# Moving the float64 loads and the converted stores of a fused attention and two-MLP kernel from SyncE's queue to ScalarE's, with the conversion's sum in place

## The chip, the cores and the metric

The kernel runs on one core of a Trainium2 chip. The metric is the device time of one execution in microseconds (us), and lower is better. The core has TensorE (PE, with its weight loads as PEld), VectorE (DVE), ScalarE (ACT), GpSimd (POOL) and SyncE (SP), which run their own instruction lists in order and wait for one another by semaphores. DMAs are started by an instruction in the list of an engine; before the change that engine is SP for all of them.

## The reference

An attention with pooled queries is followed by two MLPs over the same 2304 tokens, batch by batch. q, k and v are float32; the four weight matrices are float64.

```python
# batch, n_heads, seq, head_dim = 4, 8, 1152, 64
q_pool = q.reshape(B, H, S // factor, factor, D).mean(axis=3)     # factor = 2
scores = scale * np.matmul(q_pool, k.transpose(0, 1, 3, 2))
scores = scores - np.max(scores, axis=-1, keepdims=True)
attn = np.exp(scores)
attn = attn / (np.sum(attn, axis=-1, keepdims=True) + 1e-09)
return np.matmul(attn, v).astype(np.float32)
...
# moe:  d_model, d_ff = 512, 2048
h = x @ w_in
g = np.maximum(0.01 * h, h)
return (g @ w_out).astype(np.float32)
...
# moe2: same shapes
g = np.where(h > 0.0, h, alpha * (np.exp(np.minimum(h, 0.0)) - 1.0))
return (g @ w_out).astype(np.float32)
```

## The kernel before

Matrix products are made from float32r halves: a float32 operand is split into a high and a low part (`psplit`: the high part by ACT or DVE, the low part by POOL or DVE as a subtraction), and three products (high-high, high-low, low-high) are accumulated where both operands are split. The attention of one pair of heads is nine score tiles: scores on PE (L452), a row maximum on DVE (L457, L459), the exponential on ACT (L463, with the row sum), transposes on PE (L475), a split of the transposed tile by ACT (L261) and DVE (L267), and the product with v (L496). One MLP of one batch runs over 16 blocks `f` of 128 hidden columns: `up` (L629) makes h for one block and the two halves of 288 tokens, ACT and DVE apply the activation (L640 and L642, or L645, L648 and L650), ACT and POOL split it into `g`, and after every fourth block `down` (L667) multiplies by w_out and DVE adds into `acc` (L680).

**Weights.** Every MLP block needs one 128x512 piece of w_in and one of w_out. The first batch of each layer converts them from float64; the later batches reload the converted float32 pieces, which the first stored to DRAM (`kept`). There are 2 layers x 16 blocks x 2 pieces = 64 pieces, and `convert` handles each in two halves of 256 columns, so 128 blocks. For one block: SP loads 256 columns as pairs of 32-bit words into `cr` (L290); DVE makes two passes over the high words into a buffer `ct` (L293, L296); ACT scales the low words in place (L299) and takes the magnitude into `cm` (L301); POOL adds the low part to `ct` (L303); DVE multiplies `ct` by a mask made from `cm` and writes the half of the piece, `wr` (L305). `cr`, `ct` and `cm` have two buffers each (CB). When a piece is complete SP stores it (L328), ACT splits it into the matmul's weight `wi` or `wo` (L261) and POOL makes the low part (L267). `wr` has four buffers, two per block `f`. The five output tiles at the end of each batch also use the tag `cr` for the ACT evictions (L707) that SP then stores (L712).

**Order.** Nothing is in hand order: each step is added to `Program` with an engine, a cost in ns and a rank, and `schedule` lays all steps out with these costs and fixed latencies (a DMA from SP counts 60 ns and lands 2500 ns later; three matmuls of an MLP block count 3 x 123 ns). An engine takes the step of lowest rank that is ready by that plan, and the instructions are written out in the order of the planned starts. On the chip every engine then follows its list in order, whatever the real durations are. In the lists below, `w0_6_0` is the stored piece of layer 0, block 6, w_in (`_1` for w_out), and the numbers behind the names are those of buffers.

Of the kernel before, what the change touches and what calls it, by code (L numbers as in the profile page):

```python
# [36 lines left out]
class Program:  # L37
# [10 lines left out]
    def __init__(self):  # L48
        self.ops, self.tags = [], {}

# [5 lines left out]

    def add(self, engine, cost, rank, fn, w=(), r=()):

        me = len(self.ops)
        deps, starts, frees = set(), set(), []  # L60

        def hits(accesses, part):
            return [o for o, p in accesses if p is None or part is None or p == part]

        for x in r:
            b, part = x if isinstance(x, tuple) else (x, None)
            deps.update(hits(b.writers, part))
            b.readers.append((me, part))
        for x in w:
            b, part = x if isinstance(x, tuple) else (x, None)  # L70
            deps.update(hits(b.writers, part))
            deps.update(hits(b.readers, part))
            if b.first is None:
                b.first = me
            if b.prev is not None:
                frees.append(b.prev)
            if b.before is not None:
                starts.add(b.before)
            b.writers.append((me, part))
        deps.discard(me)  # L80
        self.ops.append((engine, cost, rank, fn, deps, starts, frees))

    def schedule(self):
# [25 lines left out]
        while left:  # L109
# [4 lines left out]
            while again:  # L114
                again = False
                for e in idle:
# [16 lines left out]
                    for o, done in out[i]:  # L133
# [5 lines left out]
                        else:  # L139
                            t = end + self.LATENCY.get(e + " " + e2, self.LATENCY[e])  # L140
                        ready[o] = max(ready[o], t)
                        need[o] -= 1
# [12 lines left out]
def kernel(  # L155
# [36 lines left out]
    CW = 256  # L192
    CB = 2
    CLEAD = 3
# [76 lines left out]
    def convert(rank, dst, src):  # L271
# [6 lines left out]
        for n in range(0, 512, CW):  # L278
            r = sb("cr", [128, CW, 2], U32, CB)
            t = sb("ct", [128, CW], U32, CB)  # L280
            mag = sb("cm", [128, CW], F32, CB)

            def load(n=n, r=r):
                rv = r.ap.rearrange("p n t -> p (n t)")
                if len(src.shape) == 3:
                    k0, kn = n // src.shape[2], CW // src.shape[2]
                    rv, sv = rv.rearrange("p (c n) -> p c n", c=kn), src[:, k0:k0 + kn, :]
                else:
                    sv = src[:, n:n + CW]
                nc.sync.dma_start(out=rv, in_=sv.bitcast(U32))  # L290

            prog.add("SP", 60, rank - 1, load, w=[r])
            prog.add("DVE", dve(CW, True), rank, lambda r=r, t=t: V.tensor_scalar(  # L293
                out=t.ap, in0=r[:, :, 1], scalar1=3, scalar2=0x3FFFFFF8,
                op0=ALU.logical_shift_left, op1=ALU.bitwise_and), w=[t], r=[(r, 1)])
            prog.add("DVE", dve(CW), rank, lambda r=r, t=t: V.scalar_tensor_tensor(  # L296
                out=t.ap, in0=r[:, :, 1], scalar=0xC0000000, in1=t.ap,
                op0=ALU.bitwise_and, op1=ALU.bitwise_or), w=[t], r=[(r, 1), t])
            prog.add("ACT", act(CW, sbuf=True), rank, lambda r=r: A.activation(  # L299
# [3 lines left out]
            prog.add("POOL", pool(CW), rank, lambda t=t, r=r: G.tensor_tensor(  # L303
                out=t.ap, in0=t.ap, in1=r[:, :, 0], op=ALU.add), w=[t], r=[t, (r, 0)])
            prog.add("DVE", dve(CW), rank, lambda n=n, t=t, mag=mag: V.scalar_tensor_tensor(  # L305
                out=dst[:, n:n + CW], in0=mag.ap, scalar=MIN_HI, in1=t.ap.bitcast(F32),
                op0=ALU.is_ge, op1=ALU.mult), w=[(dst, n)], r=[t, mag])

    kept = {}

    def load_w(rank, layer, w_in, w_out, f):

        src = (w_in[:, f * 128:(f + 1) * 128].rearrange("(c p) f -> p c f", p=128),
               w_out[f * 128:(f + 1) * 128, :])
        rs = [sb("wr", [128, 512], F32, WRB) for _ in range(2)]
        for i, r in enumerate(rs):
            if w_in.dtype == F32:
# [7 lines left out]
            else:  # L325
                convert(rank - CLEAD, r, src[i])
                kp = kept[layer, f, i] = Buf(lambda i=i: dram.tile([128, 512], F32, name=f"w{layer}_{f}_{i}"))
                prog.add("SP", 60, rank, lambda r=r, kp=kp: nc.sync.dma_start(out=kp.ap, in_=r.ap), w=[kp], r=[r])  # L328
        wi = sb("wi", [128, 2, DC, 128], F32R, WIB)
        wo = sb("wo", [128, 2, DM], F32R, WOB)  # L330
        psplit(rank - 0.5, WH, WL, lambda: wi[:, 0].rearrange("p c n -> p (c n)"),
               lambda: wi[:, 1].rearrange("p c n -> p (c n)"), lambda: rs[0].ap, 512, (wi, 0), [rs[0]])
        psplit(rank - 0.5, WH, WL, lambda: wo[:, 0], lambda: wo[:, 1], lambda: rs[1].ap, 512, (wo, 0), [rs[1]])
        return wi, wo

# [259 lines left out]
    def mlp(at, span, b, layer, xin, w_in, w_out, tags):  # L595
# [22 lines left out]
        def up(f):  # L618
# [4 lines left out]
            for hf in range(2):  # L623
# [9 lines left out]
                for c in range(DC):  # L633
                    prog.add("PE", 3 * 123, rank + step * hf / 2, lambda h=h, c=c, cols=cols: mm(h, c, cols),
                             w=[h], r=[wi, (xs[c], hf), (xs[c], 2 + hf)])
# [21 lines left out]
        def down(fc):  # L657
            for hf in range(2):
                for d in range(DC):
# [12 lines left out]
                    for f in fs:  # L672
                        prog.add("PE", 3 * 123, rank, lambda f=f, mm=mm: mm(f), w=[y],
                                 r=[w[f][1], (g[f], hf), (g[f], 2 + hf)])
# [94 lines left out]
```

## Time and profile before

| | us |
|---|---|
| median of 3 runs | 1546.47 |
| lowest and highest | 1545.47, 1552.09 |
| the profiled execution's own time | 1545.34 |
| its span, first to last instruction | 1543.5 |
| PE busy (share of the span) | 1414.5 (92%) |
| ACT busy | 1065.9 (69%) |
| DVE busy | 1011.4 (66%) |
| POOL busy | 830.3 (54%) |
| mean busy share of the 16 DMA engines, queue of SP | 28.0% |

The shares are means over stages that differ. The core starts with attention of the first batch and the first conversions; from about 216 to 593 us the two MLPs of the first batch run, with the conversions of the rest of the weights and the attention of the next batch between them; from 606 us on only reloaded weights are used. The chain of work that ended last is PE for 64% of the span and DVE for 21%.

### The profile page before, as it was taken

The page shows a single profiled execution, that of the slowest core. Times are in us where ns is not written, and L with a number is a line of the kernel's source. Part 1 is how long each engine was busy: PE and PEld are TensorE (multiplying, and loading weights), DVE is VectorE, ACT ScalarE, POOL GpSimd, SP SyncE. Part 2 cuts the span into 40 slices and gives each one's busy share as a digit, 9 for nine tenths or more (in the row PEclk, how much of TensorE's full clock was granted, in tenths as well). Part 3 has the DMA queues.
Part 4 walks back from the last instruction along what each step waited for, and adds up shares of the span by engine and source line. Part 5 has one row for each costly group of instructions (what it writes and reads, how often), then busy time and mean ns, then how long its engine had stood idle before and what let it go on. Part 6 is the DMA issues. An engine that isn't in the chain of part 4 may idle for free.

```text
span 1543.5 us, 28953 instructions
## 1 busy us (share of the span) xinstructions
PE 1414.5 (92%) x10288; PEld 1365.2 (88%) x10288; DVE 1011.4 (66%) x2273; ACT 1065.9 (69%) x2901; POOL 830.3 (54%) x840
## 2 busy tenths in 40 slices
PE   5878889888888898999999999999999999899997
PEld 4777788888878887999999999899999998899897
DVE  6999889899998998556565556645665554124222
ACT  6989878776678787676668776676667763443553
POOL 5443255765766667254555556254554445466662
PEclk9999999999999999999999999999999999999999
DMA  4332123343334443222222222222221121322221
GB/s 138 99 115 87 40 75 123 121 130 125 126 118 144 130 143 120 74 71 73 67 69 86 79 78 63 74 76 66 71 67 59 55 56 56 93 76 82 69 82 39
DMA packets 82642, 135.59 MB, mean 88 GB/s; under 512 B 8512, under 2 KB 26944, under 8 KB 82496
## 3 DMA queue, kind: packets, MB, share of 16 engines
q1 hardware_dynamic: 82496, 133.73, 28.0%
q8 instruction: 81, 1.33, 0.4%
q14 instruction: 65, 0.53, 0.1%
HBM read 112.20 MB, written 21.50 MB: 87 GB/s over the span
## 4 chain that ended last, share of the span: by engine, by line
PE 64%; DVE 21%; ACT 6%; issue 3%; DMA 3%; POOL 2%; SPq 0%; ACTq 0%; POOLq 0%; DVEq 0%
PE h L667 17%; PE h L629 16%; PE s L452 8%; PE o L496 7%; PE t L475 5%; DVE m L457 3%; PE s L629 3%; DVE ct L293 3%; DVE wr L305 3%; DVE ct L296 3%; DVE pt L267 2%; PE s L667 2%; PE t L373 2%; PE t L629 2%; PE t L667 2%
## 5 line engine op out<-in xcount | busy, mean ns | idle before, releaser
L667 PE MATMUL h<-g,wo 128*128 128x288 f32 x2544 | 437.1, 302 | 17.5 <-DVE t L650 7.9
L629 PE MATMUL h<-xs,wi 128*128 128x288 f32 x2520 | 429.2, 305 | 22.9 <-DVE t L650 14.2
L629 PEld LDWEIGHTS h<-xs,wi 128*128 128x128 f32 x2520 | 362.5, 190 | 32.5 <-DVE t L650 20.0
L667 PEld LDWEIGHTS h<-g,wo 128*128 128x128 f32 x2544 | 367.1, 188 | 23.8 <-DVE t L650 9.6
L457 DVE TENSOR_REDUCE m<-s 128x1 f32<-128x384 f32 x432 | 232.2, 550 | 74.4 <-PE s L452 71.6
L261 ACT ACTIVATE pt<-t 128x384 fp32r<-128x384 f32 (+1 forms) x416 | 184.0, 457 | 115.2 <-PE t L475 108.3
L463 ACT ACTIVATE p<-s,m 128x384 f32<-128x384 f32 x432 | 249.5, 588 | 18.3 <-DVE m L459 18.0
L267 DVE TENSOR_TENSOR pt<-t,pt 128x384 fp32r<-128x384 f32 (+1 forms) x416 | 206.8, 509 | 73.3 <-ACT pt L261 71.7
L267 POOL TENSOR_TENSOR g<-t,g 128x288 fp32r<-128x288 f32 x256 | 211.1, 831 | 79.9 <-ACT g L261 75.5
L267 POOL TENSOR_TENSOR wo<-wr,wo 128x512 fp32r<-128x512 f32 x128 | 166.4, 1304 | 137.5 <-ACT wo L261 134.3
L452 PE MATMUL s<-kT,qT 128*128 128x384 f32 x768 | 197.0, 354 | 25.4 <-ACT p L463 24.5
L267 POOL TENSOR_TENSOR wi<-wr,wi 128x512 fp32r<-128x512 f32 x128 | 167.6, 1309 | 91.9 <-ACT wi L261 79.3
L496 PE MATMUL o<-pt,vn 128*128 128x256 f32 (+1 forms) x1152 | 192.5, 303 | 5.5 <-DVE pt L267 3.6
L475 PE MATMUL t<-ident,p 128*128 128x128 f32 x1116 | 181.6, 277 | 12.4 <-DVE pt L267 11.7
L496 PEld LDWEIGHTS o<-pt,vn 128*128 128x128 f32 x1152 | 165.5, 190 | 10.6 <-DVE pt L267 10.2
L475 PEld LDWEIGHTS t<-ident,p 128*128 128x128 f32 x1116 | 139.4, 142 | 22.1 <-DVE pt L267 12.3
L452 PEld LDWEIGHTS s<-kT,qT 128*128 128x128 f32 x768 | 125.5, 192 | 32.2 <-ACT p L463 31.0
L303 POOL TENSOR_TENSOR ct<-ct,cr 128x256 uint32<-128x256 uint32 x128 | 98.8, 774 | 96.7 <-DVE ct L296 29.8
L261 ACT ACTIVATE g<-t 128x288 fp32r<-128x288 f32 x256 | 112.2, 445 | 49.0 <-DVE t L650 28.4
L267 POOL TENSOR_TENSOR vn<-raw,vn 128x576 fp32r<-128x576 f32 x32 | 46.4, 1449 | 174.4 <-ACT vn L261 174.4
L261 ACT ACTIVATE wo<-wr 128x512 fp32r<-128x512 f32 x128 | 80.6, 630 | 78.9 <-PE h L667 47.5
L680 DVE TENSOR_TENSOR acc<-h,acc 128x288 f32<-128x288 f32 x158 | 71.1, 452 | 67.2 <-PE h L667 66.1
(106 smaller groups left out, 2080.0 us busy)
## 6 DMA issues: line engine op xcount, KB each, us to landing
wr<-w SPq DMA_DIRECT2D x192, 256.0 KB, 2.6
cr<-in_moe_w_in_dram SPq DMA_DIRECT2D x64, 256.0 KB, 2.7
cr<-in_moe_w_out_dram SPq DMA_DIRECT2D x64, 256.0 KB, 2.7
w<-wr SPq DMA_DIRECT2D x64, 256.0 KB, 2.4
raw<-in_k_dram SPq DMA_DIRECT2D x32, 288.0 KB, 3.0
raw<-in_v_dram SPq DMA_DIRECT2D x32, 288.0 KB, 3.1
raw<-in_q_dram SPq DMA_DIRECT2D x32, 256.0 KB, 2.9
out_dram<-cr SPq DMA_DIRECT2D x16, 256.0 KB, 2.1
```

The costliest lines, as they stand in the source:

```text
L261: prog.add("ACT", act(n, sbuf=not psum), rank, lambda: A.activation(out=hi(), in_=src(), func=ACTF.Copy), w=[w], r=r)
L267: lambda: eng.tensor_tensor(out=lo(), in0=src(), in1=f32(hi()), op=ALU.subtract),
L293: prog.add("DVE", dve(CW, True), rank, lambda r=r, t=t: V.tensor_scalar(out=t.ap, in0=r[:, :, 1], scalar1=3, scalar2=0x3FFFFFF8, op0=ALU.l ...
L303: prog.add("POOL", pool(CW), rank, lambda t=t, r=r: G.tensor_tensor(out=t.ap, in0=t.ap, in1=r[:, :, 0], op=ALU.add), w=[t], r=[t, (r, 0)])
L452: PE.matmul(out=st[:, 0:384], lhsT=qa(a), rhs=kT[:, 384 * c:384 * c + 384], start=(i == 0), stop=(i == len(seq) - 1))
L457: prog.add("DVE", dve(384), rank - LR, lambda st=st, c=c: V.tensor_reduce(out=m[:, c:c + 1], in_=st[:, 0:384], axis=AX.X, op=ALU.max), w=[ ...
L463: prog.add("ACT", act(384, True), rank - LE, lambda c=c: A.activation(out=p[:, 384 * c:384 * c + 384], in_=banks[c][:, 0:384], func=ACTF.E ...
L475: PE.transpose(out=t[:, i, :], in_=p[:, (3 * c + i) * 128:(3 * c + i + 1) * 128], identity=ident)
L496: PE.matmul(out=o[:, 0:n], lhsT=vn[:, c, :], rhs=pt[th][:, a, c % 3, :], start=(c == 3 * ORDER[0] and a == 0), stop=(c == 3 * ORDER[2] + 2 ...
L629: PE.matmul(out=h[:, 0:HB], lhsT=wi[:, a, c, :], rhs=xs[c][:, e, cols], start=(c == 0 and a == 0 and e == 0), stop=(c == DC - 1 and a == 1))
L667: PE.matmul(out=y[:, 0:HB], lhsT=w[f][1][:, a, d * 128:(d + 1) * 128], rhs=g[f][:, e, cols], start=(f % FC == 0 and a == 0 and e == 0), st ...
L680: prog.add("DVE", dve(HB), rank - HURRY, lambda y=y, a_=a_, cols=cols: V.tensor_tensor(out=a_[:, cols], in0=y[:, 0:HB], in1=a_[:, cols], o ...
```

## The change

Three things move, and some of the planner's numbers.

- The load of a float64 block and the store of a converted piece are issued from ACT's list rather than SP's. The planner counts 80 ns of ACT for each, and takes their result as ready 3000 ns later than an ACT result would be (`late`). The store's rank goes from `rank` to `rank - 0.4`, behind the two splits of the same block (`rank - 0.5`), and it is added behind them.
- The buffer `ct` is gone: both DVE passes, the POOL sum and the mask work in the half of `wr` itself. `wr` is thus first written by the first pass and not by the last step.
- `CB` is 3 and not 2: three `cr` buffers, for the loads and for the output tiles. `cm` keeps two.
- Three matmuls of an MLP block count 3 x 133 ns in the planner, in `up` and in `down`, where they counted 3 x 123.

```diff
-    def add(self, engine, cost, rank, fn, w=(), r=()):
+    def add(self, engine, cost, rank, fn, w=(), r=(), late=0):
...
+        if late:
+            self.late[me] = late
...
-                        ready[o] = max(ready[o], t)
+                        ready[o] = max(ready[o], t + self.late.get(i, 0) * done)
...
-    CB = 2
+    CB = 3
...
             r = sb("cr", [128, CW, 2], U32, CB)
-            t = sb("ct", [128, CW], U32, CB)
-            mag = sb("cm", [128, CW], F32, CB)
+            t = lambda n=n: dst[:, n:n + CW].bitcast(U32)
+            mag = sb("cm", [128, CW], F32, 2)
...
-                nc.sync.dma_start(out=rv, in_=sv.bitcast(U32))
-
-            prog.add("SP", 60, rank - 1, load, w=[r])
+                nc.scalar.dma_start(out=rv, in_=sv.bitcast(U32))
+
+            prog.add("ACT", 80, rank - 1, load, w=[r], late=3000)
...
             prog.add("POOL", pool(CW), rank, lambda t=t, r=r: G.tensor_tensor(
-                out=t.ap, in0=t.ap, in1=r[:, :, 0], op=ALU.add), w=[t], r=[t, (r, 0)])
+                out=t(), in0=t(), in1=r[:, :, 0], op=ALU.add), w=[(dst, n)], r=[(dst, n), (r, 0)])
...
-                prog.add("SP", 60, rank, lambda r=r, kp=kp: nc.sync.dma_start(out=kp.ap, in_=r.ap), w=[kp], r=[r])
+                stores.append((kp, r))
...
+        for kp, r in stores:
+            prog.add("ACT", 80, rank - 0.4, lambda r=r, kp=kp: nc.scalar.dma_start(out=kp.ap, in_=r.ap), w=[kp], r=[r],
+                     late=3000)
...
-                    prog.add("PE", 3 * 123, rank + step * hf / 2, lambda h=h, c=c, cols=cols: mm(h, c, cols),
+                    prog.add("PE", 3 * 133, rank + step * hf / 2, lambda h=h, c=c, cols=cols: mm(h, c, cols),
...
-                        prog.add("PE", 3 * 123, rank, lambda f=f, mm=mm: mm(f), w=[y],
+                        prog.add("PE", 3 * 133, rank, lambda f=f, mm=mm: mm(f), w=[y],
```

Two places of the lists show the move. First SP in the middle of the conversions, around blocks 8 and 9 of the first layer; before, the loads of float64 blocks (L290), the loads of k, q and v (L349, `raw`) and the stores of pieces (L328) stand in one row:

```order
L328 DMA w0_8_0_3545<-wr_3490 128x512
L290 DMA cr_3578<-in_moe_w_in_dram 128x2x256
L349 DMA raw_3622<-in_k_dram 128x576
L349 DMA raw_3624<-in_q_dram 128x512
L290 DMA cr_3635<-in_moe_w_in_dram 128x2x256
L328 DMA w0_8_1_3742<-wr_3722 128x512
L290 DMA cr_3770<-in_moe_w_out_dram 128x512
L290 DMA cr_3787<-in_moe_w_out_dram 128x512
L349 DMA raw_3826<-in_v_dram 128x576
L328 DMA w0_9_0_3901<-wr_3887 128x512
```

In the changed kernel SP has at this place only the loads of the attention (the line is now L357):

```order
L357 DMA qrem_3032<-in_q_dram 64x128 x2
L357 DMA raw_3463<-in_v_dram 128x576
L357 DMA raw_3660<-in_k_dram 128x576
L357 DMA raw_3664<-in_q_dram 128x512
L357 DMA raw_3904<-in_v_dram 128x576
L357 DMA raw_4270<-in_k_dram 128x576
```

What left SP's list stands in ACT's. Here is ACT around block 6 before, between the conversion steps (L299, L301), exponentials (L463), splits (L261) and evictions:

```order
L299 ACTIVATE cr_3205<-cr_3205 128x256
L301 ACTIVATE cm_3272<-cr_3205 128x256
L261 ACTIVATE pt_3275<-t_3175 128x3x64
L261 ACTIVATE pt_3029<-t_3253 128x3x64
L463 ACTIVATE p_3243,sum_2704<-s_3181,m_3155 128x384
L261 ACTIVATE pt_3295<-t_3253 128x3x64
L261 ACTIVATE wi_3297<-wr_3128 128x512
L507 ACTIVATE tm_3319<-o_3236 64x320
L299 ACTIVATE cr_3279<-cr_3279 128x256
L301 ACTIVATE cm_3333<-cr_3279 128x256
```

The same place after, where the loads (L293) stand between compute steps and the conversion steps are L302 and L304:

```order
L302 ACTIVATE cr_3192<-cr_3192 128x256
L293 DMA cr_3278<-in_moe_w_out_dram 128x512
L471 ACTIVATE p_3255,sum_2673<-s_3137,m_3127 128x384
L293 DMA cr_3284<-in_moe_w_out_dram 128x512
L304 ACTIVATE cm_3287<-cr_3192 128x256
L515 ACTIVATE tm_3293<-o_3194 64x320
L293 DMA cr_3299<-in_moe_w_in_dram 128x2x256
L471 ACTIVATE p_3255,sum_2673<-s_3166,m_3127 128x384
L264 ACTIVATE pt_3177<-t_3289 128x3x128
L685 ACTIVATE acc_3316<-h_3235 128x288
L264 ACTIVATE pt_3239<-t_3301 128x3x128
L264 ACTIVATE wi_3326<-wr_3079 128x512
```

A load in ACT's list now stands before an exponential or an eviction, which cannot start on ACT until the load has been issued.

## Rows read from the trace of the kernel before

**Rows 1.** The page: busy time by engine, then busy tenths in 40 slices.
```profile
PE 1414.5 (92%) x10288; PEld 1365.2 (88%) x10288; DVE 1011.4 (66%) x2273; ACT 1065.9 (69%) x2901; POOL 830.3 (54%) x840
...
DVE  6999889899998998556565556645665554124222
```
**Rows 2.** Windows: stretch and length; busy us of PE, PEld, DVE, ACT, POOL; clock; DMA.
```profile
0.00:165.00 165.00, 125.10 (x832) 112.91 (x832) 142.59 (x349) 139.67 (x396) 73.28 (x83) 0.97 0.33 104
...
216.00:593.00 377.00, 328.63 (x2313) 307.07 (x2312) 351.62 (x746) 289.36 (x816) 245.41 (x259) 0.99 0.41 130
...
606.00:1543.00 937.00, 905.89 (x6756) 894.45 (x6755) 465.08 (x1060) 583.22 (x1542) 485.35 (x475) 0.99 0.24 70
```
**Rows 3.** Waits of SP's queue, 216 to 593 us: waiter, releaser, us in total, times, longest.
```profile
SPq L290 <- POOL ct L303: 158.7, 102, 4.2
SPq L290 <- ACT cm L301: 52.9, 40, 3.8
```
**Rows 4.** The float64 loads and the stores: issue ns min/median/max; us to landing.
```profile
L290 SPq DMA_DIRECT2D cr<-in_moe_w_in_dram x64: 378/379/587, 4.7 to 578.9; - x64
L290 SPq DMA_DIRECT2D cr<-in_moe_w_out_dram x64: 327/328/579, 13.2 to 585.5; - x64
...
DMA to landing us min/median/max: 2.4/2.7/4.7
...
L328 SPq DMA_DIRECT2D w<-wr x64: 320/327/535, 25.1 to 593.9; - x64
```
**Rows 5.** Chain of waits that ended last within 216 to 593 us, by line.
```profile
by line: DVE ct L296 10.2%; DVE wr L305 10.0%; DVE ct L293 10.0%; issue 7.7%; DVE m L457 7.4%; DVE pt L267 5.7%; PE h L667 4.7%; PE h L629 4.2%; DMA cr<-in_moe_w_out_dram 3.7%; DMA cr<-in_moe_w_in_dram 3.3%; POOL ct L303 2.6%; DVE acc L680 
```
**Rows 6.** DVE's groups, 216 to 593 us: busy us, mean ns | idle before, releasers.
```profile
L305 DVE SCALAR_TENSOR_TENSOR wr<-cm,ct 128x256 f32<-128x256 f32 x107 | 74.3, 698 | 1.5 <-POOL ct L303 1.4
L296 DVE SCALAR_TENSOR_TENSOR ct<-cr,ct 128x256 uint32<-128x256 uint32 x106 | 69.0, 654 | 0.9
L293 DVE TENSOR_SCALAR ct<-cr 128x256 uint32<-128x256 uint32 x106 | 56.6, 537 | 3.6 <-DMA cr<-in_moe_w_in_dram 1.8 <-DMA cr<-in_moe_w_out_dram 1.6
L267 DVE TENSOR_TENSOR pt<-t,pt 128x384 fp32r<-128x384 f32 (+1 forms) x114 | 56.2, 504 | 2.9 <-ACT pt L261 2.7
...
L642 DVE TENSOR_TENSOR t<-h,t 128x288 f32<-128x288 f32 x29 | 13.0, 447 | 5.7 <-ACT t L640 5.7
```
**Rows 7.** ACT's conversion step, 216 to 593 us, in the same form.
```profile
L299 ACT ACTIVATE cr<-cr 128x256 uint32<-128x256 uint32 x104 | 45.8, 440 | 15.3 <-DMA cr<-in_moe_w_out_dram 11.3 <-DMA cr<-in_moe_w_in_dram 2.7 <-POOL wi L267 0.9
```
**Rows 8.** DVE's conversion steps, whole run: ns min/median/max.
```profile
L293 DVE TENSOR_SCALAR ct<-cr x128: 273/294/1514, 7.7 to 589.7; 128x256 uint32<-128x256 uint32 x128
...
L305 DVE SCALAR_TENSOR_TENSOR wr<-cm,ct x128: 402/417/1685, 12.6 to 593.3; 128x256 f32<-128x256 f32 x128
```
**Rows 9.** Timeline around 301 us: start us, us, engine, line (ACT, DVE, POOL).
```profile
301.43 0.43 ACT L301 ACTIVATE cm<-cr 128x256 f32<-128x256 f32 x1
...
304.18 0.43 ACT L299 ACTIVATE cr<-cr 128x256 uint32<-128x256 uint32 x1
304.51 0.42 ACT L301 ACTIVATE cm<-cr 128x256 f32<-128x256 f32 x1
...
301.19 1.51 DVE L293 TENSOR_SCALAR ct<-cr 128x256 uint32<-128x256 uint32 x1
...
300.95 1.61 POOL L267 TENSOR_TENSOR kn<-raw,kn 128x576 fp32r<-128x576 f32 x1
...
303.64 0.74 POOL L303 TENSOR_TENSOR ct<-ct,cr 128x256 uint32<-128x256 uint32 x1 [0.75 <-issue]
```
**Rows 10.** Waits in the first 165 us: waiter, releaser, us in total, times, longest.
```profile
POOL qs L397 <- DMA raw<-in_q_dram: 14.6, 5, 4.0
...
DVE ct L293 <- DMA cr<-in_moe_w_in_dram: 7.0, 4, 5.9
```
**Rows 11.** Timeline: output tiles at 642 us (PE behind the evictions) and at the end.
```profile
644.52 3.71 PE L629 MATMUL h<-xs,wi 128*128 128x288 f32 x15 [1.79 <-ACT cr L707]
...
1538.79 0.60 ACT L707 ACTIVATE cr<-t 128x512 f32<-128x512 f32 x1 [1.49 <-DMA out_dram<-cr]
```

More of the change, by code (lines that the diff above doesn't have):

```diff
@@ L48, in __init__ @@
     def __init__(self):
-        self.ops, self.tags = [], {}
+        self.ops, self.tags, self.late = [], {}, {}
     def buf(self, tag, bufs, make):
@@ L289, in load @@
                     sv = src[:, n:n + CW]
-                nc.sync.dma_start(out=rv, in_=sv.bitcast(U32))
-            prog.add("SP", 60, rank - 1, load, w=[r])
+                nc.scalar.dma_start(out=rv, in_=sv.bitcast(U32))
+            prog.add("ACT", 80, rank - 1, load, w=[r], late=3000)
             prog.add("DVE", dve(CW, True), rank, lambda r=r, t=t: V.tensor_scalar(
-                out=t.ap, in0=r[:, :, 1], scalar1=3, scalar2=0x3FFFFFF8,
-                op0=ALU.logical_shift_left, op1=ALU.bitwise_and), w=[t], r=[(r, 1)])
+                out=t(), in0=r[:, :, 1], scalar1=3, scalar2=0x3FFFFFF8,
+                op0=ALU.logical_shift_left, op1=ALU.bitwise_and), w=[(dst, n)], r=[(r, 1)])
             prog.add("DVE", dve(CW), rank, lambda r=r, t=t: V.scalar_tensor_tensor(
-                out=t.ap, in0=r[:, :, 1], scalar=0xC0000000, in1=t.ap,
-                op0=ALU.bitwise_and, op1=ALU.bitwise_or), w=[t], r=[(r, 1), t])
+                out=t(), in0=r[:, :, 1], scalar=0xC0000000, in1=t(),
+                op0=ALU.bitwise_and, op1=ALU.bitwise_or), w=[(dst, n)], r=[(r, 1), (dst, n)])
             prog.add("ACT", act(CW, sbuf=True), rank, lambda r=r: A.activation(
@@ L303, in convert @@
             prog.add("POOL", pool(CW), rank, lambda t=t, r=r: G.tensor_tensor(
-                out=t.ap, in0=t.ap, in1=r[:, :, 0], op=ALU.add), w=[t], r=[t, (r, 0)])
+                out=t(), in0=t(), in1=r[:, :, 0], op=ALU.add), w=[(dst, n)], r=[(dst, n), (r, 0)])
             prog.add("DVE", dve(CW), rank, lambda n=n, t=t, mag=mag: V.scalar_tensor_tensor(
-                out=dst[:, n:n + CW], in0=mag.ap, scalar=MIN_HI, in1=t.ap.bitcast(F32),
-                op0=ALU.is_ge, op1=ALU.mult), w=[(dst, n)], r=[t, mag])
+                out=dst[:, n:n + CW], in0=mag.ap, scalar=MIN_HI, in1=t().bitcast(F32),
+                op0=ALU.is_ge, op1=ALU.mult), w=[(dst, n)], r=[(dst, n), mag])
     kept = {}
@@ L315, in load_w @@
         rs = [sb("wr", [128, 512], F32, WRB) for _ in range(2)]
+        stores = []
         for i, r in enumerate(rs):
```

## The prediction

> **What bounds the kernel now.** I read the page first: PE is busy for 92% of the span, DVE for 66%, but the slices show DVE at eight to nine tenths and more for the first 15 of 40 and far lower after [rows 1]. So there are two kernels in one. From 606 us on PE is busy 905.9 of 937 us and hardly anything else can matter [rows 2]. Before that DVE is the fuller engine: in the stretch from 216 to 593 us, in which the two MLPs of the first batch run beside the conversions, DVE is busy 351.6 of 377 us (93%), PE 328.6 (87%), ACT 289.4 (77%) [rows 2]. The change touches this stretch, so I took the other views for it alone. The chain of waits there is DVE work in its majority: the three conversion steps L293, L296 and L305 are 30% of it, loads of `cr` 7.0% (26 us), "issue" 7.7% [rows 5]. Of DVE's groups the same three are the costliest, and DVE has in all only 377 - 351.6 = 25.4 us of idle time; 3.6 us of it stands before L293 and ends with a load [rows 6]. ACT waits for the same loads longer: 14.0 us before L299 [rows 7].
>
> SP's own waits say why loads come late. Of the 106 loads in the stretch, 102 waited for POOL's L303, the last reader of the `cr` buffer, 158.7 us in total, and 40 for ACT's L301 [rows 3]. With two buffers a load cannot go out before the block two places ahead is through, and it lands 2.7 us after its issue [rows 4]. The loop of the conversion is thus closed through the buffers, and SP does nothing but wait in it.
>
> **The conversions, 216 to 593 us.** A third `cr` buffer takes a load out of this loop: it can go out one block earlier, and a block takes 377/106 = 3.6 us, more than the landing of 2.7. So the waits for loads should go: 3.6 us on DVE and 14.0 on ACT. DVE's gain is more than its own 3.6, since it waits for ACT steps that stand behind the late L299: 5.7 us before L642 and 2.7 before L267 [rows 6]. 3.6 + 5.7 + 2.7 = 12.0, and I take **-12 us**. The bounds are 0, if DVE's stops merely move to its next wait, and -25, all its idle time. What is late next is DVE itself: its work in the stretch is not shortened by the change. The sum in place removes no instruction; it exchanges `ct` for `wr` in the same five steps. It makes `wr` taken earlier, at the first pass. In the list of the changed kernel the first pass on a `wr` stands behind the store of the piece that held it by 60 and more in the numbers of the buffers, which rise along the lists, so I price that at 0, up to +10 if the store is late.
>
> **The issue on ACT.** 192 issues leave SP and enter ACT's list, 128 loads and 64 stores. On SP one took 379, 328 or 327 ns [rows 4], so 64 x (379 + 328 + 327) = 66 us, some 54 of them in the stretch (106 loads, 53 stores). That is the upper bound, if nothing else of ACT goes on meanwhile. The lower bound is 0: ACT's steps overlap already, as L299 at 304.18 takes 0.43 us and L301 starts 0.33 us after it [rows 9], and an issue of 0.33 to 0.38 us that runs while the step ahead of it works costs next to nothing. The trace has no DMA on ACT, so I cannot tell; I take 0.1 us each, 19 us of ACT's time, nearer the lower end, since ACT is mostly fed and has 88 us of idle time in the stretch. A tenth of that on the path makes **+2 us** (0 to +20). The Trainium skill (Advanced Engine Details and Errata, Engine Queue Depths) gives ScalarE a queue of 8 instructions. By it the issue would be hidden nearly always, and the term would be 0 rather than +2; no row here shows the depth.
>
> **The waits on ACT.** A load still waits for POOL's sum on the buffer, and now ACT stands still for it; behind it are queued exponentials, splits and evictions, for which PE and DVE wait. One block shows the size: L301 ends at 301.86, and POOL's sum (the next L303) ends at 304.38, 2.5 us later [rows 9]. In the changed list the load stands a median of 7 ACT rows behind the last ACT step on the buffer; at 377/816 = 0.46 us a row that is 3.2 us, so the typical load finds the buffer free, but some 30 of 125 stand 5 rows or fewer behind and would wait half a microsecond or so: 15 us of ACT, part of it instead of other waits. I take **+2 us** on the path (0 to +33; the upper end is the rival below). The stores stand behind the splits of the same piece, and only a few of them wait for anything but an old DMA: 0.
>
> **The two engines on one port.** L293 takes 273 ns at best and 537 on average in the stretch, L305 402 and 698 [rows 6, 8], and the row at 301.19 shows how: it lasts 1.51 us, to 302.70, and POOL's L267, begun before it, ends at 302.56 [rows 9]. For three steps (L296 goes like L305) the excess is 106 x (264 + 251 + 296) = 86 us. The Trainium skill (SBUF — State Buffer, Who interferes with whom) tells of an exclusive lock that DVE and GpSimd take in turns, held for a whole instruction; the trace agrees, with 1.51 us for a step of 0.27. What follows from the rows: POOL's 245.4 us of work [rows 2] fill 65% of 377 us, and 68% of 361. So the excess rises with the share, 86 x 68/65 = 90: **+2 us** after what is hidden (-20 to +20, since another order meets other POOL steps).
>
> **The first 216 us, the output tiles, the planner.** SP without float64 loads in its list can fetch q, k and v sooner: POOL waits 14.6 us for q [rows 10], off the chain mostly; against that, three loads from ACT now compete with the first k. **-2 us** (-8 to +2). The third buffer lets an output tile be evicted without waiting for the store two tiles ahead: 1.79 us of PE at 644 us and 1.49 of ACT near the end [rows 11], together **-3 us** (-5 to 0). The cost of 133 in place of 123 changes the plan's idea of PE; behind 606 us, where PE has 31 us of idle time [rows 2], the order of the large groups reads nearly the same, and up to 593 us some nine row maxima fewer stand between the conversions, and come back later. 0 (-5 to +5).
>
> **The sum**, against the profiled execution's own time (span 1543.5 and 1.8 around it, 1545.3): -12 + 2 + 2 + 2 - 2 - 3 = -11, so 1534. The median of the runs, 1546.5, is 1.1 above the profiled execution, so I predict 1535.
>
> **The rivals.**
> *ACT becomes the bound* (slower). If the issues cost their full 54 us in the stretch and each load holds ACT for half of what SP waited (158.7/102/2 = 0.78 us, 83 us for 106), ACT needs 289 + 54 + 83 = 426 us where the stretch has 377: +49. It decides from 88 us in 159 transfers, 0.55 us each, on. Half of it falls into waits that ACT has anyway: +25, with -5 from the other terms 1566. For it: ACT is in order, and 102 of 106 loads waited. Against it: the third buffer and the rows in between.
> *No change.* DVE stays the bound at 93% and only its own 3.6 us and the output tiles are gained, against 4 of ACT: about 1543. The Trainium skill (DMA: Bandwidth & Descriptors, Issuing engines are not separate DMA queues) speaks for it: another issuing engine saves only the sequencer's time to issue. What the rows show is that SP's time is waiting for buffers, not issuing [rows 3], so the second list by itself would give nothing here, and the buffer all.
> *More.* All of DVE's idle time is filled (-25) and the steps meet POOL less often (a quarter of 86 is -20, half of it on the path): 1545 - 35 - 5 = 1510 at the far end, 1518 as its middle.
>
> **How the numbers follow.** Forecast (1526 to 1538) 0.40, more 0.15, no change (1538 to 1553) 0.27, ACT as the bound 0.18. Half a percent, 7.7 us, is about what a measurement of this kernel can tell from no change: faster 0.55, same 0.27, slower 0.18. The range 1512 to 1554 leaves out the end of "more" (0.05) and most of the slow rival (0.14).
>
> **What would show it.** Right: waits of L296 and L302 (the old L293 and L299) for loads near zero; DVE at 95% or more in a stretch some 12 us shorter; ACT's loads issued without long idle time behind them. Wrong: ACT rows behind a load that wait for POOL, 40 us and more in sum; or the stretch as long as before with DVE's waits moved to ACT steps; or the stretch shorter and the time given back behind 606 us, which would be the planner's order. The forecast rests most on DVE's stops being due to late loads by way of ACT.

## The result and the profile after

The changed kernel takes 1558.58 us (1554.74 to 1563.18, 8 runs), the kernel before in the same comparison 1546.64 us. The ratio is 1.0077, with a 95% interval of 1.0055 to 1.0100: 12 us **slower**, where 1535 us were forecast, and 4.6 us outside the range. The profiled execution took 1554.74 us, the lowest of the eight, so its trace (a span of 1553.0 us, 1543.5 before) shows 9.5 of the 12 us. In the code after the change the lines are 3 to 8 higher, the store's 12: loads L293, passes L296 and L299, ACT's steps L302 and L304, POOL's sum L306, mask L308, stores L340.

The page of the changed kernel, busy time by engine, then the queues (q10 is ACT's), beside [rows 1]:

```profile
PE 1422.0 (92%) x10288; PEld 1363.4 (88%) x10288; DVE 1021.3 (66%) x2273; ACT 1069.9 (69%) x2901; POOL 831.0 (54%) x840
...
q1 hardware_dynamic: 46656, 83.38, 18.3%
q10 hardware_dynamic: 35840, 50.34, 10.1%
```

The same stretches as in [rows 2], in windows of the changed kernel:

```profile
0.00:165.00 165.00, 122.43 (x797) 109.51 (x797) 143.02 (x331) 134.12 (x376) 69.19 (x78) 0.97 0.32 100
216.00:593.00 377.00, 328.69 (x2256) 301.44 (x2254) 345.06 (x735) 289.72 (x803) 245.62 (x258) 0.99 0.41 129
606.00:1543.00 937.00, 913.53 (x6827) 899.61 (x6826) 479.73 (x1082) 590.15 (x1569) 492.95 (x483) 1.00 0.24 70
```

From 216 to 593 us DVE is idle for 31.9 us, where it was 25.4, and PE has done 2256 matmuls where it had done 2313. Equal times are not equal work, so here are windows cut at the same piece of work, the first `up` matmul of the first MLP block (202.0 us before, 209.2 after), of the 17th, which is layer 1's first (422.6, 430.7), of the 29th (578.9, 594.1) and of the last batch's first (1302.0, 1311.2), found by counting the line's matmuls, 24 a block. First the kernel before:

```profile
0.00:142.00 142.00, 105.30 (x682) 94.70 (x682) 123.53 (x301) 118.39 (x337) 65.68 (x77) 0.96 0.35 111
142.00:202.00 60.00, 50.59 (x365) 46.59 (x366) 49.35 (x120) 52.45 (x150) 18.16 (x18) 1.00 0.18 53
202.00:422.60 220.60, 194.81 (x1377) 182.71 (x1376) 202.16 (x437) 166.38 (x467) 139.05 (x146) 0.98 0.36 118
422.60:578.90 156.30, 135.36 (x954) 125.67 (x952) 146.73 (x308) 123.61 (x349) 103.90 (x109) 1.00 0.42 135
578.90:1302.00 723.10, 702.70 (x5259) 693.28 (x5259) 428.94 (x978) 502.56 (x1356) 371.68 (x363) 1.00 0.24 72
```

And the changed kernel:

```profile
0.00:142.00 142.00, 104.55 (x682) 93.73 (x682) 121.67 (x284) 116.94 (x330) 61.11 (x70) 0.98 0.31 96
142.00:209.20 67.20, 52.88 (x367) 47.79 (x367) 58.34 (x133) 55.05 (x156) 21.34 (x23) 0.97 0.24 75
209.20:430.70 221.50, 192.54 (x1345) 175.94 (x1343) 205.12 (x444) 168.26 (x466) 143.87 (x150) 1.00 0.41 128
430.70:594.10 163.40, 142.85 (x956) 131.29 (x956) 147.03 (x310) 127.34 (x353) 103.71 (x111) 0.97 0.40 126
594.10:1311.20 717.10, 703.75 (x5276) 694.03 (x5277) 424.05 (x965) 499.11 (x1352) 368.04 (x358) 1.00 0.24 71
```

The loss stands in two places: 7.2 us at the end of the first attention, where DVE has 133 instructions to do instead of 120 (conversions that it had done earlier before: 284 instructions and not 301 in the first 142 us), and 7.1 us in the second half of the conversions. Later 6.0 us come back. In another execution of the same order (e1, below) the two places lose 10.8 and 5.4 us. The stretch between the two places is only 0.9 us longer, but PE does 1345 matmuls in it and not 1377, so work is put off there too: at the 134 ns that a matmul takes from 606 us on (905.9 us for 6756 [rows 2]) the 32 are some 4 us, an estimate.

In the second place the granted clock is 0.97 where it was 1.00, which is some 5 us of 163.4 (an estimate from the two numbers), and PE is busy for 7.5 us more with 956 matmuls than it was with 954. Over the whole execution the clock is no lower than before (0.992, before 0.990), and a loss stands at this place without it: the kernel before with 133 in the planner (e6, below) needs 168.4 us for the same twelve blocks at 1.00, with 27 matmuls more than before in them.

```profile
421.60:590.00 168.40, 140.26 (x981) 128.99 (x980) 155.43 (x322) 130.53 (x366) 105.28 (x110) 1.00 0.39 127
```

So the clock is not what makes the 12 us, but how much of the 7.1 is its share is not shown.

DVE's waits in the changed kernel, 216 to 593 us (waiter, releaser, us in total, times, longest), which answer to [rows 6], and ACT's conversion step, which answers to [rows 7]:

```profile
DVE m L465 <- PE s L460: 12.1, 16, 1.8
DVE pt L270 <- ACT pt L264: 6.1, 8, 2.3
DVE wr L308 <- POOL wr L306: 3.6, 8, 1.1
DVE t L658 <- ACT t L656: 3.0, 3, 1.5
```
```profile
L302 ACT ACTIVATE cr<-cr 128x256 uint32<-128x256 uint32 x105 | 46.1, 439 | 2.0 <-POOL wr L306 0.9 <-issue 0.7 <-DMA cr<-in_moe_w_out_dram 0.2
```

The waits for loads are gone, as forecast: 3.6 us on DVE and 14.0 on ACT have become none and 0.2. But DVE now waits 12.1 us for scores, and 6.1 for ACT's splits. Before, its waits for scores there came to 5.7 us:

```profile
DVE t L642 <- ACT t L640: 5.7, 3, 2.5
DVE m L457 <- PE s L452: 5.7, 12, 0.9
```

ACT has a new wait as well. With the loads early, its magnitude step now stands until a mask has freed one of the two `cm` buffers, whose number the change left as it was; from the first `up` of the first block to that of the 29th, the changed kernel and then the kernel before:

```profile
ACT cm L304 <- DVE wr L308: 12.1, 17, 1.9
```
```profile
ACT cm L301 <- DVE wr L305: 3.4, 4, 1.7
```

The loads and stores on ACT in the changed kernel, by line (issue ns min/median/max), beside [rows 4]:

```profile
L293 ACTq DMA_DIRECT2D cr<-in_moe_w_in_dram x64: 385/386/593, 0.7 to 572.1; - x64
L293 ACTq DMA_DIRECT2D cr<-in_moe_w_out_dram x64: 334/335/736, 1.7 to 579.4; - x64
```
```profile
L340 ACTq DMA_DIRECT2D w<-wr x64: 326/333/1615, 64.2 to 587.2; - x64
```

An issue takes as long on ACT as it took on SP, to 7 ns. What it costs ACT is in the timeline of the changed kernel near 298 us (start, us, engine, line):

```profile
298.48 0.44 ACT L304 ACTIVATE cm<-cr 128x256 f32<-128x256 f32 x1 [0.38 <-DVE wr L308]
298.49 0.33 ACTq L340 DMA_DIRECT2D w<-wr  x1
...
298.82 0.62 ACT L264 ACTIVATE wi<-wr 128x512 fp32r<-128x512 f32 x1
```

The store's 0.33 us run beside the 0.44 us of the step ahead of it, and the next step starts when the issue is over, before the step ahead has ended. This transfer, which found its buffer ready, took next to nothing from ACT.

### The profile page after: what moved, and what is told of

Same layout as the page of the kernel before. It is cut to its first block, busy times and chain, and to the rows that moved or that the text cites. A ratio compares the mean times of both kernels' runs of the same rounds, so it can differ in the third digit from the quotient of the medians.

```text
span 1553.0 us, 28812 instructions
## 1 busy us (share of the span) xinstructions
PE 1422.0 (92%) x10288; PEld 1363.4 (88%) x10288; DVE 1021.3 (66%) x2273; ACT 1069.9 (69%) x2901; POOL 831.0 (54%) x840
## 4 chain that ended last, share of the span: by engine, by line
PE 53%; DVE 7%; ACT 6%; issue 2%; POOL 1%; DMA 0%; ACTq 0%; POOLq 0%; DVEq 0%
PE h L675 16%; PE h L637 13%; PE s L460 5%; PE o L504 5%; PE t L483 4%; PE s L637 3%; PE s L675 2%; PE t L675 2%; PE t L637 2%; PE t L381 1%; DVE wr L308 1%; DVE xs L266 1%; DVE t L658 1%; ACT p L471 1%; ACT t L653 1%
## 5 line engine op out<-in xcount | busy, mean ns | idle before, releaser
L270 DVE TENSOR_TENSOR pt<-t,pt 128x384 fp32r<-128x384 f32 (+1 forms) x416 | 206.9, 508 | 70.7 <-ACT pt L264 69.0
L270 POOL TENSOR_TENSOR g<-t,g 128x288 fp32r<-128x288 f32 x256 | 209.8, 827 | 77.0 <-ACT g L264 72.8
L270 POOL TENSOR_TENSOR wo<-wr,wo 128x512 fp32r<-128x512 f32 x128 | 166.2, 1305 | 140.3 <-ACT wo L264 139.8
L270 POOL TENSOR_TENSOR wi<-wr,wi 128x512 fp32r<-128x512 f32 x128 | 168.2, 1314 | 75.5 <-ACT wi L264 64.6
L270 POOL TENSOR_TENSOR vn<-raw,vn 128x576 fp32r<-128x576 f32 x32 | 46.5, 1452 | 192.0 <-ACT vn L264 191.6
L306 POOL TENSOR_TENSOR wr<-wr,cr 128x256 uint32<-128x256 uint32 x128 | 99.1, 781 | 81.3 <-DVE wr L299 27.5
```

Of the source, the lines that this page charges most:

```text
L270: lambda: eng.tensor_tensor(out=lo(), in0=src(), in1=f32(hi()), op=ALU.subtract),
```

## The experiments

All were timed in five rounds against the kernel before, whose medians were 1543.1 to 1546.9 us. Two kinds must be told apart. Some keep an order of the planner word for word and change only what lies under it; the others let the planner write a new order.

### Who issues, with the order kept

*The changed kernel's order, issued from SyncE* (e1), and *the kernel before's order, issued from ScalarE* (e2):

```diff
-                nc.scalar.dma_start(out=rv, in_=sv.bitcast(U32))
+                nc.sync.dma_start(out=rv, in_=sv.bitcast(U32))
...
-            prog.add("ACT", 80, rank - 0.4, lambda r=r, kp=kp: nc.scalar.dma_start(out=kp.ap, in_=r.ap), w=[kp], r=[r],
+            prog.add("ACT", 80, rank - 0.4, lambda r=r, kp=kp: nc.sync.dma_start(out=kp.ap, in_=r.ap), w=[kp], r=[r],
```

> The changed kernel with its plan as it is (the lists of PE, DVE, POOL and the compute steps of ACT stand in the same order as in the changed kernel), but every load of a float64 block and every store of a converted piece is issued from SP, at the place where the plan had it on ACT. Theory O (the loss comes from the new order: conversions stand later in the lists and denser) expects 1556 to 1560 us, as the change. Theory I (the loss comes from ACT issuing and waiting) expects 1545 to 1550 us.

Measured 1557.82 us (ratio 1.0087, 1.0063 to 1.0112): no difference from the changed kernel. In its order the issuing engine costs nothing; its loss lies in the order, or in what the new buffers do under it (below). In e1 no step of ACT stands behind a load any more, but its wait for `cm` is longer, from 203 to 593 us:

```profile
ACT cm L304 <- DVE wr L308: 21.1, 24, 2.1
```

The rows suggest that in the changed kernel ACT stood at its loads for time that it would else have stood at `cm`, which would explain a cost of nothing.

e2 is the same edit the other way in the kernel before:

> The kernel before with its plan as it is (same compute order), but the same loads and stores are issued from ACT, at the place where the plan had them on SP; two cr buffers and ct as before. Theory O expects 1545 to 1549 us. Theory I expects 1555 us or more: 192 issues of 0.33 to 0.39 us and the waits for buffers now stand in ACT's list.

Measured 1557.89 us (1.0092, 1.0065 to 1.0119): 12 to 14 us lost. The trace tells how, in ACT's waits from 202 to 593 us:

```profile
ACT p L463 <- POOL ct L303: 2.9, 5, 0.7
...
ACT t L645 <- POOL ct L303: 2.1, 1, 2.1
```

An exponential and an activation of an MLP use nothing that POOL's sum writes. They stand behind a load that waits for the sum to free its `cr`. Such waits of ACT come to 9.0 us for POOL's sum and 3.5 for the mask (of steps that neither read `wr` nor write `cm`); in the kernel before there is none.

*The same with three buffers* (e13). This is e9 (below: in-place sum, three `cr` buffers, transfers on SP, 1537.72 us) with its 192 transfers issued from ACT at the same places:

```diff
-                nc.sync.dma_start(out=rv, in_=sv.bitcast(U32))
+                nc.scalar.dma_start(out=rv, in_=sv.bitcast(U32))
...
-                prog.add("SP", 60, rank, lambda r=r, kp=kp: nc.sync.dma_start(out=kp.ap, in_=r.ap), w=[kp], r=[r])
+                prog.add("SP", 60, rank, lambda r=r, kp=kp: nc.scalar.dma_start(out=kp.ap, in_=r.ap), w=[kp], r=[r])
```

> The in-place version in the order that its two-buffer plan wrote, with three physical `cr` buffers, and now all 192 loads and stores issued from ScalarE at the same places of that order. Issued from SyncE this order took 1537.72 us; the kernel before, in its own order with two buffers, lost 12 us when its transfers were issued from ScalarE (1545.2 to 1557.9). Theory W (the 12 us were waits in ScalarE's list, of loads for a `cr` buffer that POOL still read): the third buffer takes them away, 1537 to 1541. Theory I (the issues themselves cost ScalarE its time): again some 12 us, 1547 to 1552. Theory T (the stores wait in ScalarE's list for VectorE's last conversion step, which the buffer does not touch): between, 1543 to 1547.

Measured 1544.70 us (1.0002, 0.9989 to 1.0016), 7 to 9 us above e9 (by the medians and by the ratios): Theory T's range. ACT's waits from 203.7 to 586.9 us:

```profile
ACT p L463 <- DVE wr L305: 3.1, 3, 1.2
...
ACT t L645 <- DVE wr L305: 2.3, 1, 2.3
```

With the third buffer the waits for POOL's sum have shrunk to 0.3 us. What is left are 12.1 us in which steps that don't read `wr` wait for the mask L305: they stand behind a store whose piece is not complete. In e9 there are none. The changed kernel puts its stores behind the splits and so has 3.5 us of these, but 9.1 for the sum and 2.3 for loads. e2 and e13 show that the issuing engine costs time in these two orders; that the waits do it, and not the issues with them, is read from the rows and not shown apart.

### The buffers

*In-place sum alone* (e4): the kernel before with `ct` replaced by the half of `wr`, two `cr` buffers, SP, 123.

```diff
-            t = sb("ct", [128, CW], U32, CB)
+            t = lambda n=n: dst[:, n:n + CW].bitcast(U32)
```

> The kernel before with the sum in place alone: no ct, the weight's buffer written from the first pass on; two cr, issue from SP, stores ahead of the splits and the planner's numbers as before. If the longer hold of the weight's buffer is the cause, 1552 to 1558 us; if not, 1545 to 1549 us.

Measured 1539.15 us (0.9960, 0.9944 to 0.9977): 6 us gained.

*A third `cr` buffer under that order* (e9). The planner sees two buffers and writes e4's order; three lie under it.

```diff
-            r = sb("cr", [128, CW, 2], U32, CB)
+            r = prog.buf("cr", 2, lambda: sp.tile([128, CW, 2], U32, tag="cr", name="cr", bufs=3))
```

> The kernel before with the sum in place, in the order that its planner makes for two cr buffers, but with three physical ones, so that SP waits less for a buffer and every list stays as it is. If loads that come too late are what stops DVE (the main term of the prediction), 1527 to 1533 us, 6 to 12 below the sum in place alone (1539 to 1540). If DVE stays full and the loads were early enough, 1537 to 1541. In e5 the same buffer with the order made for it gave 1547.6.

Measured 1537.72 us (0.9946, 0.9924 to 0.9967), within the noise of e4. This run is the test of the forecast's main term. SP's waits before loads, 216 to 593 us, in e4 and then in e9:

```profile
SPq L290 <- POOL wr L303: 140.1, 91, 6.7
```
```profile
SPq L290 <- POOL wr L303: 46.2, 36, 6.8
```

ACT's waits for loads, in e4 and then in e9:

```profile
ACT cr L299 <- DMA cr<-in_moe_w_out_dram: 9.6, 11, 2.0
ACT cr L299 <- DMA cr<-in_moe_w_in_dram: 6.8, 10, 1.9
```
```profile
ACT cr L299 <- DMA cr<-in_moe_w_out_dram: 4.0, 5, 1.4
ACT cr L299 <- DMA cr<-in_moe_w_in_dram: 2.4, 3, 1.8
```

The buffer does what it was to do: 94 us less of SP's waits for POOL's sum, 10 less of ACT's for loads, and DVE's waits for loads fall from 3.4 to 0.3 us. The windows from 216 to 593 us, e4 and then e9, show that it bought nothing: PE has done the same work.

```profile
216.00:593.00 377.00, 332.35 (x2327) 308.39 (x2326) 356.61 (x757) 292.52 (x820) 250.29 (x264) 0.99 0.42 133
```
```profile
216.00:593.00 377.00, 332.56 (x2333) 309.01 (x2332) 358.02 (x755) 291.88 (x821) 249.85 (x263) 0.99 0.41 131
```

DVE is busy for 1.4 us more and has done two instructions fewer. The two waits for ACT that the forecast added to its sum are still there, e4 and then e9:

```profile
DVE pt L267 <- ACT pt L261: 2.7, 7, 0.7
DVE t L642 <- ACT t L640: 1.0, 3, 0.5
```
```profile
DVE pt L267 <- ACT pt L261: 2.8, 8, 0.7
DVE t L642 <- ACT t L640: 1.4, 3, 0.8
```

By the forecast's rule this order had 3.4 + 1.0 + 2.7 = 7.1 us to win.

*The third buffer told to the planner* (e5, `CB = 3` on e4):

> The kernel before with the sum in place and three cr buffers (for the loads and for the output tiles); issue from SP, stores ahead of the splits and the planner's numbers as before. If the third buffer is worth what the prediction took it for, some 8 to 12 us under the sum in place alone (1539): 1527 to 1532 us. If DVE stays full all the same, 1536 to 1541. If it moves the order for the worse, as one part of the change does, over 1545.

Measured 1547.57 us (1.0008, 0.9988 to 1.0028): 7 to 8 us slower than e4, by the new order, since the buffer itself cost nothing in e4's. Here ACT's wait for `cm` is 33.2 us, where e4 has none. Whether this wait costs time is open: no run gives `cm` a third buffer.

*The changed kernel with two `cr` buffers and `ct`* (e3):

> The changed kernel with the buffers of before: two cr, two ct, the sum in ct and not in the weight's buffer; issue from ACT, the stores behind the splits and the planner's numbers as in the change. If the longer hold of the weight's buffer by the sum in place is what pushes the conversions back, 1546 to 1551 us; if the issue on ACT, the place of the stores or the planner's numbers do it, 1556 to 1562 us.

Measured 1562.75 us (1.0122, 1.0093 to 1.0151), 4 us above the changed kernel by the medians. Going back to the old buffers wins nothing in the order that the planner then writes. The new buffers are not shown to be a cause; the sum in place has no run under a kept order.

### The planner's numbers

*133 in the kernel before* (e6) and *123 in the changed one* (e12):

```diff
-                    prog.add("PE", 3 * 123, rank + step * hf / 2, lambda h=h, c=c, cols=cols: mm(h, c, cols),
+                    prog.add("PE", 3 * 133, rank + step * hf / 2, lambda h=h, c=c, cols=cols: mm(h, c, cols),
```

> The kernel before with the planner's three matmuls at 133 each and nothing else. If this number makes the order of the changed kernel cost its 12 us, 1553 to 1560 us; if it does not, 1543 to 1549.

> The changed kernel with the planner's three matmuls at 123 as before, all else as changed. If the number is a cause of its own, as before with 133 says (+7), 1549 to 1554 us. If the third buffer alone is enough to let the conversions run ahead, 1556 to 1561, since both causes then work on the same lead.

Measured 1553.82 us (1.0045, 1.0024 to 1.0067) for e6 and 1549.47 us (1.0026, 1.0014 to 1.0038) for e12. This number costs about 7 us in the kernel before and 8 to 9 in the changed one. The rest of the change costs 4 us at 123 and 5 at 133. The place of the first loss goes with that rest: the first `up` of the first block starts at 202.3 us in e6, as before (202.0), and at 212.2 in e12.

*Is that number special?* 124 in the kernel before (e11), 122 there (e15), 134 in the changed kernel (e14); each changes the planned order and nothing else.

> The kernel before with the planner's three matmuls at 124 each, where it has 123: a number nearly without meaning that moves the lists all the same. It shows how far any other order may lie from that of before. If orders of this planner scatter by little, 1545 to 1549 us; if the 7 us of the 133 run are mere scatter of orders, anything between 1535 and 1560.

> The kernel before with 3*122 in place of 3*123: only the planned order differs. Theory S: somewhere from 1536 to 1556 (124 gave 1537.5, 123 gave 1546, 133 gave 1553.8). Theory P (a larger number makes the planner run conversions further ahead, a smaller one not): 1537 to 1547, with a lead of the conversions of 20 to 30 us, and if the lead comes out above 33 us the time is 1552 or more.

> The changed kernel with the planner's number for three matmuls at 3*134 in place of 3*133: nothing is different but the order that the planner writes. Theory S (the loss is one draw from the scatter of such orders, as the 8 us that 124 in place of 123 gave in the kernel before): the time moves by several us from 1558, anywhere from 1545 to 1562. Theory P (a property of the changed plan, such as conversions run 35 us ahead of their use, costs the time in every such order): 1555 to 1562, and the lead of the conversions stays at 33 to 38 us.

Measured 1537.46 us (0.9948, 0.9929 to 0.9967), 1538.23 us (0.9954, 0.9938 to 0.9970) and 1565.72 us (1.0134, 1.0115 to 1.0152). A step of one in 123 moves the time by 7 to 9 us. So orders scatter by half a percent for no reason that is known here, and a single re-planned difference of 6 to 9 us (e4, e5, e6, e12) is a fact of that order, not yet a property of the part that was changed.

*The loads alone as planned ACT steps* (e8: e4 with cost 80 and `late=3000` for the loads, stores on SP) and *the stores behind the splits* (e7: e4 with rank - 0.4, on SP):

> The kernel before with the sum in place, and with the loads of float64 blocks as ACT steps of the planner (80 ns, result 3000 ns late, issued from ACT); stores from SP as before, two cr buffers, 123. If the issue in ACT's list costs what it did in the order of before, 1547 to 1553 us; if a plan that knows of the loads on ACT makes room for them, 1537 to 1543.

> The kernel before with the sum in place, and with the stores behind the splits (rank - 0.4, added after them), still from SP. If the late store, which holds the weight's buffer until it lands, is what pushes the conversions back, 1549 to 1556 us; if not, 1537 to 1542, as the sum in place alone.

Measured 1550.05 us (1.0020, 0.9999 to 1.0042) for e8, some 10 us above e4, and 1541.61 us (0.9965, 0.9941 to 0.9988) for e7, no difference from e4. Both are single orders, with the reservation above.

### Do conversions run too far ahead?

In the changed kernel a block's mask ends on average 34.8 us before its first `up` matmul (blocks 6 to 31), in the kernel before 24.0, in e5 and e6 37 to 38. DVE would then do early what is not needed, ahead of steps that PE waits for. A smaller `CLEAD` (e10) did not move this lead (37.3 us) and so tested nothing:

> The changed kernel with CLEAD 2 and not 3: the planner ranks every conversion one rank, about one MLP block, later. Theory M (the change lets the conversions run ahead of what PE needs, and on a full DVE they displace steps that PE waits for) expects the pace of before again, 1545 to 1552 us. If the loss is in ACT's issue or its waits, or the lead does not matter, 1556 to 1562.

Measured 1559.33 us (1.0079, 1.0058 to 1.0100). The number of `wr` buffers moves it better: three in the changed kernel (e17), five in e4 (e18).

```diff
-    WRB = 4
+    WRB = 3
```

> The changed kernel with three weight buffers `wr` in place of four, so that conversions cannot run as far ahead of the matmuls that use them. Theory P (conversions run 35 us ahead displace steps that TensorE waits for): the lead falls to 10 to 25 us and the time from 1558 to 1540 to 1550. Theory S (the order is one of a scatter and the lead is not its cause): the lead falls and the time lies anywhere from 1545 to 1566. Rival L (the lead is what covers the loads and the transfers issued from ScalarE): the lead falls, conversions come late for TensorE, and the time is 1562 to 1580.

> The in-place version (two `cr` buffers, transfers on SyncE, 1539.15 us, lead 21 us) with five weight buffers `wr` in place of four, so that conversions may run further ahead. Theory P: the lead rises to 33 us or more and the time to 1547 to 1556. Theory S: the lead rises and the time lies anywhere from 1536 to 1553. Rival L: more lead is more cover, 1532 to 1538.

Measured for e17 1550.59 us (1.0055, 1.0040 to 1.0069), with a lead of 27.6 us, and for e18 1530.73 us (0.9926, 0.9912 to 0.9939), with a lead of 28.4. With less lead the changed kernel gained 8 us by the medians, but 3 by the ratios, whose intervals overlap (1.0055 to 1.0100, 1.0040 to 1.0069): not clear of the noise. With more lead e4 gained 5 to 8, against the theory, and e3 has the shortest lead of all, 20.4 us, and is 4 us slower than the changed kernel. The lead is thus not shown to be the cause. Whether there is a best lead between, or each is one more order, stays open.

*The best try* (e16: e9 with 3 x 124):

> The in-place sum, transfers on SyncE, three physical `cr` buffers of which the planner counts two, and 3*124. If the gains of the in-place sum (7 us) and of the 124 order (9 us) were independent: 1530 to 1533. Theory S (each is a draw of an order, and a new order is a new draw): 1535 to 1547. Theory P: it follows the lead of the conversions, 1535 to 1540 if that is 20 to 30 us.

Measured 1536.70 us (0.9948, 0.9930 to 0.9967): the gains of e4 and e11 do not add. e18, the in-place sum with five weight buffers (the room that `ct` left), two `cr` buffers and all transfers on SP, is the fastest and beats both kernels, the kernel before by 11 to 12 us in the same comparison. Its DVE still waits for loads, 216 to 593 us:

```profile
DVE wr L293 <- DMA cr<-in_moe_w_in_dram: 3.9, 5, 1.4
```

## Why the prediction was wrong, point by point

- **The step that failed first: the conversions, -12.** The mechanism up to the buffer was right: loads waited for POOL's sum, and a third buffer takes most of these waits away, on SP, on ACT and on DVE (e9 against e4, and the changed kernel). That a stop of DVE is time won when it goes was not. With the order kept the time moved by 1.4 us, inside the noise, where the forecast's rule gives 7.1 for that order and gave 12 for the kernel before. The 5.7 us before L642 and 2.7 before L267 were put down to a late L299 without a row that links them; they are waits for ACT that did not go with the waits for loads (3.7 us together in e4, 4.2 in e9). In the changed kernel DVE waits 6.1 us before L270, the old L267, and 3.0 before L658, the old L650, while its waits for scores grew from 5.7 to 12.1. DVE's idle time in a stretch where it is at 93% was taken for the path; in e9 it fell by 1.4 us. The forecast's own sign of failure, "DVE's waits moved to ACT steps", came in part: in the stretch DVE waits 6.4 us more for scores, 3.5 more for POOL and 2.8 more for ACT.
- **The planner, 0 (-5 to +5).** The second failure, and as large: who issues costs nothing in the changed order (e1) and the third buffer nothing in a kept one (e9), which leaves the order (with the sum in place, which has no run under a kept order), and 133 alone is 7 us in one kernel and 8 to 9 in the other. The order of large groups behind 606 us was compared, and read as nearly the same; orders planned with one more or less in 123 differ by 7 to 9 us here (e11, e15). The term needed a range of at least that on both sides. What in the new order costs the time stays open.
- **The issue on ACT, +2 (0 to +20).** Right in size: the issues take 64 x (386 + 335 + 333) = 67 us of ACT's sequencer and cost nothing in the changed order (e1); the one near 298 us runs beside the step ahead. The Trainium skill (Advanced Engine Details and Errata, Engine Queue Depths), by whose queue of 8 instructions for ScalarE the term would be 0, agrees with this; the depth itself is shown by no row.
- **The waits on ACT, +2 (0 to +33).** The estimate was 15 us of ACT, and the trace has 9.1 + 3.5 + 2.3 = 14.9. What that costs depends on the order: nothing in the changed one; with the lists of the kernel before the issues and waits together cost 12 to 14 us (e2), with three buffers 7 to 9 (e13). For the stores 0 was right as the change puts them; at their old place they hold ACT for 12.1 us. The rival in which ACT becomes the bound came near in time (1566) but not in its mechanism: ACT is busy for 289.7 us in the stretch, as before.
- **The port, +2 (-20 to +20).** L296, L299 and L308 take 525, 622 and 713 ns, and took 537, 654 and 698: 3 us less over 106 blocks. Within the bounds. Over the whole run DVE's same 2273 instructions took 9.9 us more, 9.0 of it between 142 and 209 us, where it has 13 instructions more.
- **The first 216 us, -2 (-8 to +2).** Failed: +7.2 up to the first block. POOL's waits for q in the first 165 us are 16.1 us, not less than the 14.6 before. I looked at the fetches of q and k, and not at where the conversions of this stretch would come to stand.
- **The output tiles, -3.** Right in kind: ACT's waits there for the stores fall from 5.4 to 1.9 us in all, and the stretch that holds the later batches is 6.0 us shorter; how much of that the tiles make is not shown.
- **`wr` held earlier, 0 (0 to +10).** The in-place sum gained 6 us in the one order that has it alone (e4), and the room it leaves can hold a fifth `wr` buffer (e18). Why it gains was not settled.
- **"No change" and "more".** The argument of "no change", that a second list gives nothing and DVE stays full, is what e1 and e9 show; it lacked the order's loss. "More" fell with the step that it shares with the forecast: DVE's idle time in the stretch grew from 25.4 to 31.9 us.
- **Slips in the sums.** In "more", 1545 - 35 - 5 is 1505 and not 1510. The 361 us behind the 68% of POOL have no row; 377 - 12 = 365 gives 67%, and 89 us and not 90. 104 loads start in the stretch, not 106. None of them decides.

## What to carry to other kernels

A wait that ends most of an engine's idle time is worth its length only if what stands behind it is next on the path: put the resource under an unchanged order first (another buffer that the planner does not see), and look whether the time follows. Where a planner writes the order, an edit is two edits; time each part with the order kept, and a change of the planner's numbers that means nothing beside it, to know the scatter before a few microseconds are given a cause. A transfer issued from a compute engine cost nothing in one order here and 7 to 14 us in two others, so look at what each transfer waits for at its place in the list. The rows suggest, and no run shows in time, that stores belong behind the readers of the same data and loads behind the release of their buffer with room to spare.

## What the runs showed of the hardware that was not expected

- A DMA's issue on ACT takes the same 0.33 to 0.39 us as on SP, and the one near 298 us overlaps the ACTIVATE ahead of it. A transfer that has to wait holds the steps behind it, and the profile then names the waited-for engine at the next compute step (e2: exponentials released by POOL's sum).
- 123 ns a matmul was too little for the chip: from 606 us on PE's 6756 matmuls of all kinds took 905.9 us [rows 2], 134 ns each. The number nearer to that gave the slower order in both kernels, by no more than orders scatter.
